# Attention scores as one 64-row by 128-column matmul each, in a kernel whose other matmuls are 64 by 32

## The chip, the cores and the metric

The kernel runs on one core of a Trainium2 chip. The metric is the device time of one execution in microseconds (us). A core has TensorE (PE, with its weight loads shown apart as PEld), VectorE (DVE), ScalarE (ACT), GpSimd (POOL) and SyncE (SP, which issues the DMAs). Matmul results go to PSUM, which here is one tensor `ps` of 128 partitions by 8 banks of 512 f32.

## The reference, cut to what matters

```python
xn = _layernorm(x)                                  # x: 1 x 2048 x 512, bf16
# attention, 32 heads of 16
scores = jnp.einsum("bhqd,bhkd->bhqk", q, k) * (Dh ** -0.5)
p = _softmax(scores, axis=-1)
o = jnp.einsum("bhqk,bhkd->bhqd", p, v)             # then @ wo
# feed-forward, F = 1792
gate = einsum(xn, W_gate); up = einsum(xn, W_up)
h = gate * (gate > 0) * up                          # then @ W_down
return x + attention(xn) + feed_forward(xn)
```

## The kernel before, in words

**Tiling.** The 2048 queries are cut into 4 blocks `c4` of 512, the 32 heads into 4 groups `gg` of 8, and each group into two sets `ee` of 4 heads. The 2048 keys are cut into 16 tiles `kt` of 128. `kT` holds the keys transposed: 128 partitions are the 8 heads of a group at 16 rows each. `qT` holds the queries with the rows of the other heads set to zero, so that a product over 64 rows (4 heads) gives the scores of one head: an operation takes half of the rows of the array, 64, and writes 128 keys by 512 queries to a PSUM bank.

**Scores.** `score` (L1180) is one such operation for one head, one key tile, one query block. It is done as four weight loads of 64 rows by 32 columns (`kload`, L1189) and four matmuls of 64 by 32 (`sc`, L1193) that write 32 partitions each of the same bank. There are 2048 of these operations, 1024 on each half of the rows.

**Exponentials.** Most key tiles go through ACT: two score operations, one on each half of the rows, fill two banks, and one ACTIVATE (L1252) turns them into probabilities in `ring`; that is a unit, and there are 720. The others (`quad`, L1203) go through DVE: four score operations, each evacuated by a TENSOR_SCALAR (L1211) into `qd` as the bits of an approximate exponential, with two shifted copies made by DVE (L1230) and POOL (L1226).

**Probability times value (PV).** `pv_stream` (L1143) multiplies `v_aug` (values, and a column of ones for the sum) with the probabilities, again as four loads and four matmuls of 64 by 32 for each half, accumulated in one bank.

**The rest.** Projections (`mm_chain`, L770, with `chain_part`, L749), the feed-forward (`glu`, L907) and the output rows (`out_rows`, L941) are woven in between as four loads and four matmuls of 64 by 32 on one half. At the start and at the end some matmuls use 128 rows: transposes (128x128, L720), fillers (128x128, L1267, and 128x32, L1272) that wait for nothing, the last output rows (128x32, L1089), and sums and spreads of the last normalisation (L1051, L1062).

**Order.** Every operation is registered with `G.op`, with an engine, a planned duration (216 ns for each TensorE operation of the halves), a priority and what it reads and writes. `Graph.run` places all of them once, before launch, and so fixes the order of each engine's queue. For TensorE it tracks the two halves of the rows apart and takes operations of mode "half" on both halves side by side; a change between the modes "half", "col" and "full" has a planned cost:

```python
    SWITCH = 107.0
```

`Graph.emit` (L373) writes the queues as instructions. For TensorE it remembers for each half which weights are loaded (`held`, by `wkey`) and leaves out a load where the same weights are there already (L382 to L389). A matmul whose weights were loaded by its own instruction goes through `matmul_loaded` (L99), which passes the tile size; so all these matmuls, scores and others, carry the line L101 in the profile. An operation is four instructions of that line.

Of the kernel before, what the change touches and what calls it, by code (L numbers as in the profile page):

```python
# [95 lines left out]
                 "load", "wsrc", "wkey", "wwaits")  # L96


def matmul_loaded(e, out, w, x, start, stop, at):  # L99

    return e.add_instruction(mybir.InstMatmult(  # L101
        name=e.bass.get_next_instruction_name(), engine=mybir.EngineType.PE, ins=[e.lower_ap(x), e.lower_ap(w)], outs=[e.lower_ap(out)],
        start_tensor_calc=start, stop_tensor_calc=stop, tile_size=(64, 32), tile_position=at, ldweights=False))


class Graph:
# [266 lines left out]
    def emit(self, nc, es):  # L373
# [5 lines left out]
        sems = {c: es.enter_context(nc.semaphore("s_" + c.lower())) for c in ("PE", "PEhi", "ACT", "DVE", "POOL")}  # L379
        known = {e: {} for e in self.ENGS}  # L380

        loads, held = {}, [None, None]  # L382
        for o in self.queue["PE"]:
            if o.load is None:
                held = [None, None]
            elif held[o.half] == o.wkey:
                o.load, o.wsrc = False, ()
            else:
                held[o.half] = o.wkey  # L389
# [16 lines left out]
        while left:  # L406
            moved = False
            for e in self.ENGS:
                q = self.queue[e]
                while pos[e] < len(q):  # L410
                    o = q[pos[e]]
                    if any(d.hb is None for d in o.deps):
                        break
                    k = known[e]
# [94 lines left out]
def bass_parallel_sum__mha_block__glu_gated_reglu__prompt_kernel(  # L509
# [14 lines left out]
    with ExitStack() as es:  # L524
        def sb(name, shape, dt):
            return es.enter_context(nc.sbuf_tensor(name, shape, dt))
# [22 lines left out]
        kT = sb("kT", [128, NGG, S], BF16)  # L549
        qT = sb("qT", [128, NQ, 4, 512], BF16)  # L550
# [17 lines left out]
        ps = es.enter_context(nc.psum_tensor("ps", [128, 8, 512], FP32))  # L568
# [180 lines left out]
        def chain_part(w, x, dst, half, flags):  # L749

            def fn(e):
                start, stop = flags()
                ww, xx, d, ins = w(), x(), dst(), None
                for j in range(4):
                    c = slice(32 * j, 32 * j + 32)
                    if half is None:
                        ins = e.matmul(d[c, :], ww[:, c], xx, start=start, stop=stop, tile_position=(0, 32 * j))
                    else:
                        ins = matmul_loaded(e, d[c, :], ww[rows, c], xx[rows], start, stop, (rows.start, 32 * j))
                return ins  # L760

            def load(e):
                for j in range(4):
                    e.ldweights(w()[rows, 32 * j:32 * j + 32], tile_position=(rows.start, 32 * j))  # L764
            rows = slice(0, 128) if half is None else slice(64 * half, 64 * half + 64)
            return fn, load if half is not None else None
# [116 lines left out]
        def key_tiles(gg, kt):  # L883
            return t_k0 if gg == kt == 0 else t_k[(gg, kt // 4)]
# [110 lines left out]
        for c4 in range(NB):  # L995
            rows = []
# [12 lines left out]
        at, rest = 40.0, sum(j[1] for j in seq[:-4])  # L1009
        for w, n, fn, lead in seq:  # L1010
            at = max(at, w)
# [131 lines left out]
        def pv_stream(key, kt, src, reads, u, prio):  # L1143
# [10 lines left out]
            for half in range(2):  # L1154
                rows = slice(64 * half, 64 * half + 64)

                def vs(j, rows=rows):
                    a = VW * (8 * gg + 2 * j + ee) - DH * ee
                    return v_flat[rows, kt, a:a + 32]

                def vload(e, half=half, vs=vs):
                    for j in range(4):
                        e.ldweights(vs(j), tile_position=(64 * half, 32 * j))  # L1163

                def pv(e, half=half, vs=vs, rows=rows):
                    ins = None
                    for j in range(4):
                        ins = matmul_loaded(e, ps[32 * j:32 * j + 32, BANK[t.slot], :], vs(j), src[j](rows), st[0] == 0, st[0] == st[1] - 1, (64 * half, 32 * j))
                    st[0] += 1
                    return ins  # L1170
                o = G.op("PE", 216, pv, reads=[t_vones, t_v[kt]] + reads, joins=[t], prio=prio, name="pv%d" % u, mode="half", half=half, bank=(t, 0), slack=PV_SLACK,
                         load=vload, weights=[t_vones, t_v[kt]], wkey=("v", gg, ee, kt))
                pv_ops[key].append(o)
# [6 lines left out]
        def score(key, j, t, bank, sub, u, prio, order, urgent, joins=(), after=None):  # L1180

            c4, gg, ee, kt = key
            half, p = j // 2, j % 2
            rows, tq = slice(64 * half, 64 * half + 64), q_slot[(c4, gg)]

            def ks(m):
                return kT[rows, gg, 128 * kt + 32 * m:128 * kt + 32 * m + 32]

            def kload(e):  # L1189
                for m in range(4):  # L1190
                    e.ldweights(ks(m), tile_position=(64 * half, 32 * m))  # L1191

            def sc(e):  # L1193
                ins = None
                for m in range(4):
                    ins = matmul_loaded(e, ps[32 * m:32 * m + 32, bank(), :], ks(m), qT[rows, tq.slot, 2 * p + ee, :], True, True, (64 * half, 32 * m))
                return ins
            tq.r.append(G.op("PE", 216, sc, reads=[t_q[(c4, gg, ee)][p], key_tiles(gg, kt)], joins=[t] + list(joins), prio=prio, order=order,
                             name="sc%d" % u, mode="half", half=half, bank=(t, sub), urgent=urgent, after=after,
                             load=kload, weights=[key_tiles(gg, kt)], wkey=("k", gg, kt)))  # L1200
            return G.ops[-1]
# [38 lines left out]
        for u, unit in enumerate(units):  # L1240
# [5 lines left out]
            key, p = unit[:4], unit[4]  # L1246
# [58 lines left out]
```

## Time and profile before

| what | before |
|---|---|
| median of 2 runs (lowest to highest) | 712.56 us (710.72 to 714.4) |
| the profiled execution | 710.57 us |
| its span | 708.8 us |
| mean granted TensorE clock | 0.998 |
| TensorE matmuls | 690.8 us busy, 22224 |
| TensorE weight loads | 378.5 us busy, 20965 |
| ACT | 669.3 us busy, 728 |
| DVE | 637.0 us busy, 1055 |
| POOL | 415.6 us busy, 358 |
| score matmuls (64*32) | 8192, with 8084 weight loads |

The span runs from the first to the last instruction of the profiled execution; its own time is a little longer. Busy is the union of the instructions' times on an engine. Matmuls are pipelined: a matmul of 512 columns is shown 0.38 us long though the next of its half starts earlier, so the pace is read from the starts. In a group's line come the source line, engine, operation, tensors, tile size (rows*columns), shape and count, then busy time, mean length of one in ns, and idle time of the engine before them with what ended it.

### The profile page before, as it was taken

Reading aid. Unit: us, or ns where it says so; the run is one execution under the profiler, and the core shown is the slowest. Engines: PE = TensorE matmul, PEld = TensorE weight load, DVE = VectorE, ACT = ScalarE, POOL = GpSimd, SP = SyncE. Lnnn points to the kernel's source line nnn. Section 1 sums busy time; section 2 is a strip of 40 time slices with the busy share of each in tenths; the row PEclk is TensorE's granted clock in tenths of the full one; section 3 lists DMA queues with packets and bytes.
Section 4 is the critical chain, followed back from the end, with each engine's and each line's share of the span. In section 5 each row is a group of like instructions: output and inputs, shape, how many; then the busy total and the mean of one; then the engine's idle time right before and its main releaser. Section 6 shows DMA issues by size and latency. Waiting matters only on the chain.

```text
span 708.8 us, 46867 instructions
## 1 busy us (share of the span) xinstructions
PE 690.8 (97%) x22224; PEld 378.5 (53%) x20965; DVE 637.0 (90%) x1055; ACT 669.3 (94%) x728; POOL 415.6 (59%) x358
## 2 busy tenths in 40 slices
PE   8989999999999999999999999999999999999996
PEld 4455555555445555555555555555555465555552
DVE  8766999999999988999999999799999989999873
ACT  5799999999999999999999999999999999999972
POOL 3203654756666547758647667576566766765641
PEclk9999999999999999999999999999999999999999
DMA  7322132243221113122221112232210122122011
GB/s 208 63 64 56 37 74 57 59 129 79 56 50 32 41 49 74 40 66 52 61 61 31 35 43 68 54 72 63 62 49 23 36 53 70 42 63 63 27 30 34
DMA packets 94893, 41.22 MB, mean 58 GB/s; under 512 B 77224, under 2 KB 90728, under 8 KB 94696
## 3 DMA queue, kind: packets, MB, share of 16 engines
q1 hardware_dynamic: 94696, 38.22, 21.3%
q8 instruction: 169, 2.77, 1.7%
q14 instruction: 28, 0.23, 0.1%
HBM read 31.06 MB, written 2.35 MB: 47 GB/s over the span
## 4 chain that ended last, share of the span: by engine, by line
PE 88%; DVE 4%; DMA 2%; ACT 2%; issue 1%; SPq 1%; POOL 1%; DVEq 0%; POOLq 0%
PE ps L101 85%; ACT ring L1252 2%; DVE qd L1211 2%; SPq L812 1%; DMA rb<-rec_scr 1%; PE ps L863 1%; DVE qd L1230 1%; PE ps L1267 1%; DMA xnT<-xn_sb 1%; DMA rec_scr<-rrec 0%; DMA x_sb<-oT 0%; PE ps L1089 0%; POOL oT L1131 0%; DVE o_sb L1110 0%; DVE v_aug L829 0%
## 5 line engine op out<-in xcount | busy, mean ns | idle before, releaser
L1252 ACT ACTIVATE ring<-ps 128x1024 bf16<-128x1024 f32 x720 | 664.2, 1100 | 17.8 <-PE ps L101 16.4
L101 PE MATMUL ps<-qT,kT 64*32 64x512 bf16 x8192 | 466.3, 376 | 4.2 <-ACT ring L1252 2.0
L1211 DVE TENSOR_SCALAR qd<-ps 128x512 int16<-128x512 f32 x608 | 396.3, 684 | 30.4 <-PE ps L101 26.4
L1226 POOL TENSOR_TENSOR qd<-qd,shift 128x512 int32<-128x512 int32 x272 | 277.0, 1040 | 203.8 <-DVE qd L1230 93.8
L101 PE MATMUL ps<-qd,v_aug 64*32 64x512 bf16 x3648 | 297.9, 375 | 1.8 <-issue 1.2
L1191 PEld LDWEIGHTS <-kT 64*32 64x32 bf16 x8084 | 172.4, 91 | 160.6 <-issue 77.6
L101 PE MATMUL ps<-ring,v_aug 64*32 64x512 bf16 x2880 | 249.9, 376 | 0.4
L1163 PEld LDWEIGHTS <-v_aug 64*32 64x32 bf16 x5376 | 130.5, 91 | 68.6 <-issue 26.2
L101 PE MATMUL ps<-xnT,wgs 64*32 64x512 bf16 x1792 | 135.5, 375 | 0.0
L101 PE MATMUL ps<-xnT,wus 64*32 64x512 bf16 x1792 | 134.6, 375 | 0.3 <-issue 0.2
L1230 DVE TENSOR_SCALAR qd<-qd 128x2048 int16<-128x2048 int16 x168 | 115.8, 701 | 5.6 <-PE ps L101 5.1
L1118 POOL TENSOR_TENSOR rrec<-rsum,minus 128x16 f32<-128x16 f32 x31 | 92.0, 2967 | 36.9 <-DMA rsum<-o_sb 36.9
L764 PEld LDWEIGHTS <-hT 64*32 64x32 bf16 x1792 | 43.1, 91 | 25.4 <-issue 5.9
L101 PE MATMUL ps<-Wd,hT 64*32 64x512 bf16 x768 | 55.8, 376 | 0.6 <-DVE qd L1211 0.3
L764 PEld LDWEIGHTS <-wus 64*32 64x32 bf16 x1792 | 43.5, 91 | 20.3 <-issue 4.0
L764 PEld LDWEIGHTS <-wgs 64*32 64x32 bf16 x1792 | 43.2, 91 | 16.1 <-issue 3.6
L101 PE MATMUL ps<-Wv,hT 64*32 64x512 bf16 x512 | 41.1, 376 | 0.4 <-issue 0.4
L927 DVE SCALAR_TENSOR_TENSOR hT<-ps,up_sb 128x512 bf16<-128x512 f32 x56 | 38.3, 685 | 2.8 <-PE ps L101 2.6
L101 PE MATMUL ps<-Wk,hT 64*32 64x512 bf16 x512 | 40.5, 375 | 0.0
L923 DVE COPY up_sb<-ps 128x512 f32<-128x512 f32 x56 | 38.3, 684 | 2.0 <-PE ps L101 1.9
L101 PE MATMUL ps<-xnT,Wk 64*32 64x512 bf16 x480 | 36.0, 375 | 2.6 <-issue 1.5
L101 PE MATMUL ps<-Wo_p,x_sb 64*32 64x512 bf16 x448 | 36.5, 376 | 0.4 <-issue 0.4
(73 smaller groups left out, 287.6 us busy)
## 6 DMA issues: line engine op xcount, KB each, us to landing
rb<-rec_scr SPq DMA_DIRECT2D x31, 256.0 KB
wus<-in_B_W_up_dram SPq DMA_DIRECT2D x56, 128.0 KB, 3.1
wgs<-in_B_W_gate_dram SPq DMA_DIRECT2D x56, 128.0 KB, 3.2
xr_sb<-in_A_x_dram SPq DMA_DIRECT2D x16, 128.0 KB, 3.3
out_dram<-xn_sb SPq DMA_DIRECT2D x16, 128.0 KB, 1.7
qT<-qf SPq DMA_DIRECT2D x120, 16.0 KB, 2.6
x_sb<-in_A_x_dram SPq DMA_DIRECT2D x8, 128.0 KB, 2.8
x_sb<-oT SPq DMA_DIRECT2D x60, 16.0 KB, 2.4
```

Of the source, the lines that this page charges most:

```text
L101: return e.add_instruction(mybir.InstMatmult(name=e.bass.get_next_instruction_name(), engine=mybir.EngineType.PE, ins=[e.lower_ap(x), e.lo ...
L764: e.ldweights(w()[rows, 32 * j:32 * j + 32], tile_position=(rows.start, 32 * j))
L812: dma(lambda e, v=v, r=r: e.dma_start(qT[r, tq.slot, v, :], qf[r, tf.slot, :]), 16, reads=[tf, t_qz], writes=[], joins=[tq], prio=prio + 0 ...
L923: G.op("DVE", 603, lambda e: e.tensor_copy(up_sb[:, tup.slot, :], bank_of(tu)), reads=[tu], writes=[tup], prio=-590)
L927: G.op("DVE", 603, lambda e: e.scalar_tensor_tensor(out=hT[:, th.slot, :], in0=bank_of(tg), scalar=0.0, in1=up_sb[:, tup.slot, :], op0=ALU ...
L1118: G.op("POOL", 3060, lambda e: e.tensor_tensor(rrec[:, par, :], rsum[:, par, :], minus[:], ALU.pow), reads=[ts, t_ones], writes=[trr], pri ...
L1163: e.ldweights(vs(j), tile_position=(64 * half, 32 * j))
L1191: e.ldweights(ks(m), tile_position=(64 * half, 32 * m))
L1211: G.op("DVE", 601, lambda e, j=j, tx=tx: e.tensor_scalar(qd[:, tq.slot, 512 * j:512 * j + 512], ps[:, BANK[tx.slot], :], IBIAS[3], 0.0, op ...
L1226: G.op("POOL", POOL_NS / POOL_PIECES + 60, lambda e, x=x, c=slice(i * m, i * m + m): e.tensor_tensor(x().bitcast(I32)[:, c], raw().bitcast ...
L1230: G.op("DVE", 600, lambda e, n=n, x=x: e.tensor_scalar(x(), raw(), float(SHIFTS[n + 1]), None, op0=ALU.add), reads=[ti, tq], writes=[t], p ...
L1252: exp_ops[u] = G.op("ACT", 904, lambda e, tr=tr, k0=k0: e.activation(ring[:, tr.slot, :, :], ps[:, 4 * k0:4 * k0 + 2, :], ACTF.Exp, scale= ...
```

## The change

The scores alone are made with a tile of 64 rows by 128 columns: one weight load of 128 keys, and one matmul that writes all 128 partitions of the bank. `matmul_loaded` gets the number of columns as an argument, with 32 for all other callers. `emit` forgets which weights are held on both halves wherever the queue passes from a score to another operation or back, so that the first operation on a half after it loads its weights anew. What the planner sees of each operation is as before.

```diff
-def matmul_loaded(e, out, w, x, start, stop, at):
+def matmul_loaded(e, out, w, x, start, stop, at, cols=32):
...
-        start_tensor_calc=start, stop_tensor_calc=stop, tile_size=(64, 32), tile_position=at, ldweights=False))
+        start_tensor_calc=start, stop_tensor_calc=stop, tile_size=(64, cols), tile_position=at, ldweights=False))
...
-        loads, held = {}, [None, None]
+        loads, held, size = {}, [None, None], None
         for o in self.queue["PE"]:
+            wide = isinstance(o.wkey, tuple) and o.wkey[0] == "k"
+            if wide != size:
+                held, size = [None, None], wide
             if o.load is None:
...
-            def ks(m):
-                return kT[rows, gg, 128 * kt + 32 * m:128 * kt + 32 * m + 32]
+            def ks():
+                return kT[rows, gg, 128 * kt:128 * kt + 128]
 
             def kload(e):
-                for m in range(4):
-                    e.ldweights(ks(m), tile_position=(64 * half, 32 * m))
+                e.ldweights(ks(), tile_position=(64 * half, 0))
 
             def sc(e):
-                ins = None
-                for m in range(4):
-                    ins = matmul_loaded(e, ps[32 * m:32 * m + 32, bank(), :], ks(m), qT[rows, tq.slot, 2 * p + ee, :], True, True, (64 * half, 32 * m))
-                return ins
+                return matmul_loaded(e, ps[:, bank(), :], ks(), qT[rows, tq.slot, 2 * p + ee, :], True, True, (64 * half, 0), 128)
```

## The prediction

> **What bounds the kernel now.** I read the page's busy table first, then its chain, then the costliest groups. All are lines of the page of before.
>
> ```profile
> PE 690.8 (97%) x22224; PEld 378.5 (53%) x20965; DVE 637.0 (90%) x1055; ACT 669.3 (94%) x728; POOL 415.6 (59%) x358
> ...
> PE 88%; DVE 4%; DMA 2%; ACT 2%; issue 1%; SPq 1%; POOL 1%; DVEq 0%; POOLq 0%
> ...
> L1252 ACT ACTIVATE ring<-ps 128x1024 bf16<-128x1024 f32 x720 | 664.2, 1100 | 17.8 <-PE ps L101 16.4
> L101 PE MATMUL ps<-qT,kT 64*32 64x512 bf16 x8192 | 466.3, 376 | 4.2 <-ACT ring L1252 2.0
> ...
> L101 PE MATMUL ps<-qd,v_aug 64*32 64x512 bf16 x3648 | 297.9, 375 | 1.8 <-issue 1.2
> L1191 PEld LDWEIGHTS <-kT 64*32 64x32 bf16 x8084 | 172.4, 91 | 160.6 <-issue 77.6
> ```
>
> TensorE (PE) carries 88% of the chain that ended last, though ACT and DVE are also over 90% busy. A busy PE is not a full PE, so its work must be counted in slots. The timeline shows how a slot looks (start, length, engine, line, shape, count):
>
> ```profile
> 299.70 0.38 PE L101 MATMUL ps<-xnT,wus 64*32 64x512 bf16 x4
> 299.71 0.38 PE L101 MATMUL ps<-ring,v_aug 64*32 64x512 bf16 x4
> 299.92 0.38 PE L101 MATMUL ps<-xnT,wus 64*32 64x512 bf16 x4
> 299.93 0.38 PE L101 MATMUL ps<-qd,v_aug 64*32 64x512 bf16 x4
> ...
> 300.36 0.38 PE L101 MATMUL ps<-ring,v_aug 64*32 64x512 bf16 x4
> 300.39 0.56 PE L101 MATMUL ps<-qT,kT 64*32 64x512 bf16 x8
> 300.61 0.38 PE L101 MATMUL ps<-xnT,wus 64*32 64x512 bf16 x4
> 300.79 0.38 PE L101 MATMUL ps<-qT,kT 64*32 64x512 bf16 x4
> 300.82 0.38 PE L101 MATMUL ps<-qd,v_aug 64*32 64x512 bf16 x4
> ```
>
> The array works as two halves of 64 rows. Four matmuls of 64x32 start together on a half and fill it; the half takes its next four 0.216 us later (299.70 to 299.92). The 0.38 us is length with latency, not pace. The halves run different things at the same time: a projection beside a probability-times-value (PV) product, or (300.61, 300.79) a score beside a projection. This sharing is what the change touches.
>
> **An account of before in slots.** The kernel has 2752 half-width operations per half, 1024 of them scores: 2752 x 0.2157 = 593.6 us of stream. Of the span of 708.8 us that leaves 115 us. By the stretches of the trace, from 60 to 680 us (20,268 matmuls, 8 to a slot, 546.5 us of stream) 73.5 us are lost between slots; the start, the end and the few other matmuls take the remaining 41.7.
>
> **The change, part by part.**
>
> *The stream.* One matmul of 128 columns streams the same 512 elements as four of 32 beside each other: still one slot on its half. No gain. 6144 matmul instructions go. The four starts of an operation lie some 5 ns apart (first to fourth record), so 1024 scores per half could give 0 to 5 us. I take 0, since the matmuls wait on "issue" for only 4.5 us in the whole trace.
>
> *The weight load.* 8084 loads of 91 ns, four beside each other, become at most 2048 of 128 columns; a 128-column load of the transposes is 98 ns in the trace. It hides under the previous slot of 216 ns as now. Taken as 0; without that cover it is 0.1 us per score, which is what the next term measures. The PV operations that skip a load because the weights are held (288 of 1632) will load again after each change of size: also inside the next term.
>
> *The change of tile size.* This is new: a size of 64x128 between sizes of 64x32. Before has 14 changes of size, at start and end. From the timeline of the end:
>
> ```profile
> 696.09 0.60 PE L101 MATMUL ps<-ring,v_aug 64*32 64x512 bf16 x8
> 696.62 0.40 PE L1089 MATMUL ps<-Wo_p,x_sb 128*32 128x512 bf16 x4
> ...
> 698.14 0.39 PE L1089 MATMUL ps<-Wo_l,x_sb 128*32 128x512 bf16 x4
> 698.46 0.39 PE L101 MATMUL ps<-ring,v_aug 64*32 64x512 bf16 x4
> 698.78 0.62 PE L1272 MATMUL ps<-zeros 128*32 128x512 bf16 x8
> ```
>
> Slots without a change follow at 0.216 us; those with one at 0.32 (698.14 to 698.46 to 698.78), and the two slots from 696.09 take 0.53. A change costs 0.104 us, load of the new weights included. These rows change the number of rows, ours only the columns. The nearest row for columns alone:
>
> ```profile
> 699.38 0.97 PEld L1051 LDWEIGHTS ps<-selp,o_sb 128*128 128x128 f32 x8 [0.47 <-DVE o_sb L1047]
> ...
> 700.36 0.10 PEld L1272 LDWEIGHTS ps<-zeros 128*32 128x32 bf16 x4
> ```
>
> The eight loads come every 0.112 us, the last at 700.15; the filler behind them waits for nothing and could load at 700.26, but does at 700.36: 0.10 us late, for 128 to 32 columns on the same rows. One instance, with small f32 matmuls, so weak; it says that columns count. The bounds are 0 and 0.104 us for each change; I take 0.104, the row it is nearest to.
>
> How many changes? The planner fixes TensorE's order before launch, and the diff alters no duration, mode, priority or dependence that it sees, so the order stays. Along that queue the 2048 scores fall into 1026 stretches (429 with one score on each half, 315 with a single score, 266 with three, 16 longer). With the other stretches that makes 2055 changes, 2041 more than now: 2041 x 0.104 = 212 us.
>
> *The sharing lost.* If a change empties the array, a score can no longer run beside a 64x32 product. Each stretch then takes as many slots as its fuller half: 1315 for the scores instead of 1024, and 2188 for the other 3456 operations instead of 1728. Together 3503 against 2752: 751 x 0.2157 = 162 us.
>
> *Issue.* In a stretch the second half starts 13 ns after the first (two groups of loads and matmuls, as at 12.46 us). About half of the stretches feel it: some 12 us.
>
> *What is given back.* Of the 73.5 us lost between slots, part is waiting for ACT, DVE and the other half, and that has more room when the slots spread. All or nothing of it: 0 to 73.5. I take half, 37 us. ACT starts an exponential every 0.904 us at its fastest, 720 x 0.904 = 651 us, so it stops being near the bound; a score then waits behind TensorE's own order. DVE, POOL and the DMA queues issue what they did and have more time for it. The wait of a score for its PSUM bank, with all of TensorE's queue behind it, should get shorter, since the bank was read 1.1 us after the score two units earlier and a unit will take about 1.4 us.
>
> Sum: 708.8 + 212 + 162 + 12 - 37 = 1058 us of span. The profiled execution took 710.57 us, 1.8 more than its span, and is 0.3% under the median of 712.56. Forecast 1060 us. Its own range: 1020 with all the loss given back, 1097 with none, 20 us either way for 10 ns on each change: 1000 to 1115.
>
> The Trainium skill, "TensorEngine Tiling (Array Packing)", Key Properties, lists 64x128 and 64x32 as separate modes and says that a change of mode, not of tile alone, drains TensorE. By it the sum above stands even for columns alone, where the trace has a single weak row; without any drain it would be some 710.
>
> **Rivals.**
>
> *Each half changes by itself.* A half that turns to 64x128 pays, the other goes on in 64x32. For it: the halves run unrelated work and differ in their start by any offset in the timeline. Against it: the changes that the trace shows always involve all rows, so it can't tell. A half has 1413 or 1471 changes in its own order: some 1442 x 0.104 = 150 us, no sharing lost, 0 to 73.5 given back: 786 to 860, say 840 us. The Trainium skill, "TensorE: Matmul & The Clock Gate", Part 3, speaks for it: it describes loads that overlap running matmuls as long as the row groups differ, a concurrency of each sub-array.
>
> *No cost at all (the other side).* The column width is only a mask, and 64x128 mixes freely with 64x32. Then nothing on the path changes: 705 to 716, say 711 us; and if the 73.5 us between slots come partly from issue, 12,000 instructions fewer at 1.6 ns each (the spacing of records in a group) would give up to 20 us back: 690. It decides from the point where a change costs below 5 ns. Against it are the 0.10 us at 700.36 and the 4.5 us of "issue" waits.
>
> *No two 64x128 matmuls at once.* If the two halves can't both run at this width, the scores take 2048 slots instead of 1315: 733 x 0.2157 = 158 us more, 1218 us. No row speaks for it.
>
> *The edit has no effect* would show as 64*32 scores; the tile size is passed directly, so I leave it out.
>
> **How the numbers follow.** Array emptied at each change: 0.63. Each half by itself: 0.16. No cost: 0.13, of which 0.04 is a gain over 2%. No two at once: 0.05. Something in between, mostly slower: 0.03. A difference of 2% is about what a measurement of this kernel can tell from none. Slower over 2%: 0.63 + 0.16 + 0.05 + 0.02 = 0.86; within 2%: 0.09 + 0.01 = 0.10; faster: 0.04. The range takes in the first two cases and what lies between and a little above, and leaves out "no cost" and most of "no two at once": 800 to 1150 us.
>
> **What would show it.** Right: 2048 matmuls of 64*128 in the groups; a score starting 0.32 us after the last other product and never inside the slot of one; PE over 90% of the chain, ACT's exponentials still some 0.9 us long at best but only about 60% to 75% busy, and fewer waits for ACT. A score that overlaps a 64*32 slot on the other half proves the first rival or the second: the first if the same half shows gaps of 0.32, the second if 0.216. Score pairs 0.2 us apart prove the third. I am wrong in the mechanism if the time is below 900 us, in a size only if it is between.

## The result and the profile after

The changed kernel takes 1013.62 us (median of 2 runs, 1013.57 to 1013.68) against 712.56 us: a ratio of 1.42, 95% interval 1.41 to 1.44. The profiled execution has a span of 1011.9 us at a granted clock of 0.997. The forecast was 1060 us.

From the page of the changed kernel, in the order of the lines shown of before (busy, chain, groups):

```profile
PE 1002.3 (99%) x16080; PEld 276.4 (27%) x15081; DVE 667.7 (66%) x1055; ACT 737.4 (73%) x728; POOL 417.2 (41%) x358
...
PE 98%; DVE 1%; ACT 1%; issue 0%; DVEq 0%; ACTq 0%
...
L1251 ACT ACTIVATE ring<-ps 128x1024 bf16<-128x1024 f32 x720 | 732.3, 1024 | 252.7 <-PE ps L101 241.0
...
L101 PE MATMUL ps<-qT,kT 64*128 64x512 bf16 x2048 | 462.3, 385 | 1.6 <-ACT ring L1251 0.9
...
L1193 PEld LDWEIGHTS <-kT 64*128 64x128 bf16 x2040 | 102.7, 93 | 380.1 <-issue 376.3
L1166 PEld LDWEIGHTS <-v_aug 64*32 64x32 bf16 x5536 | 108.9, 90 | 177.2 <-issue 157.5
```

TensorE has 6144 matmuls and 5900 loads fewer to do and is busy 311 us longer with it. It carries 98% of the chain instead of 88%. ACT waited 16.4 us for TensorE before and waits 241.0 now: nothing beside TensorE bounds the kernel any more. The new number to see is the idle time of the weight loads of the scores: 376 us ended by "issue", that is by nothing that the profile shows, against 77.6 before. Loads that used to slip under the running slot now stand still until the array is ready.

The timeline of the changed kernel shows why (start, length, engine, line, shape, count):

```profile
420.12 0.39 PE L101 MATMUL ps<-ring,v_aug 64*32 64x512 bf16 x4
420.13 0.39 PE L101 MATMUL ps<-xnT,wus 64*32 64x512 bf16 x4
420.34 0.38 PE L101 MATMUL ps<-qd,v_aug 64*32 64x512 bf16 x4
420.35 0.38 PE L101 MATMUL ps<-xnT,wus 64*32 64x512 bf16 x4
420.67 0.39 PE L101 MATMUL ps<-qT,kT 64*128 64x512 bf16 x1
420.99 0.39 PE L101 MATMUL ps<-xnT,wus 64*32 64x512 bf16 x4
421.30 0.39 PE L101 MATMUL ps<-qT,kT 64*128 64x512 bf16 x2
421.63 0.39 PE L101 MATMUL ps<-qd,v_aug 64*32 64x512 bf16 x4
421.64 0.39 PE L101 MATMUL ps<-xnT,wgs 64*32 64x512 bf16 x4
421.85 0.38 PE L101 MATMUL ps<-ring,v_aug 64*32 64x512 bf16 x4
```

Inside a stretch of one size the step is still 0.22 us (420.12 to 420.34). Across a change it is 0.32 (420.35 to 420.67 to 420.99 to 421.30 to 421.63). And the score at 420.67 stands alone, with the other half of the rows idle; so does the projection at 420.99. In before the other half went on with its own work under a score.

By the records of the whole trace: matmuls of the two widths on 64 rows change over 2047 times, and from the last start before a change to the first start after it takes 0.305 us at least and 0.322 us at most in 19 of 20 cases. All sum up to 645.1 us, mean 0.3151. The new weights are loaded at the end of that step: the first load of the new size starts 0.304 to 0.315 us after the last start of the old one in 9 of 10 cases, and its matmul some 0.006 us behind it. The load of the score at 420.67:

```profile
420.66 0.09 PEld L1193 LDWEIGHTS <-kT 64*128 64x128 bf16 x1 [0.42 <-issue]
```

By these records the price lies ahead of the load, not in its 0.09 us. No run changes the size without a new load, so a share of the load in the price is not ruled out.

### The profile page after: what moved, and what is told of

Its sections match the earlier page's. It is cut to its first block, busy times and chain, and to the rows that moved or that the text cites. A ratio compares the mean times of both kernels' runs of the same rounds, so it can differ in the third digit from the quotient of the medians.

```text
span 1011.9 us, 34839 instructions
## 1 busy us (share of the span) xinstructions
PE 1002.3 (99%) x16080; PEld 276.4 (27%) x15081; DVE 667.7 (66%) x1055; ACT 737.4 (73%) x728; POOL 417.2 (41%) x358
## 4 chain that ended last, share of the span: by engine, by line
PE 98%; DVE 1%; ACT 1%; issue 0%; DVEq 0%; ACTq 0%
PE ps L101 96%; ACT ring L1251 1%; PE ps L866 0%; PE ps L1266 0%; PE ps L1092 0%; DVE xn_sb L1083 0%; DVE xn_sb L701 0%; DVE xnT L739 0%; PE ps L760 0%; PE ps L1054 0%; PE ps L879 0%; PE ps L723 0%; PE ps L1271 0%; DVE v_aug L832 0%; DVE qd L1210 0%
## 5 line engine op out<-in xcount | busy, mean ns | idle before, releaser
L1251 ACT ACTIVATE ring<-ps 128x1024 bf16<-128x1024 f32 x720 | 732.3, 1024 | 252.7 <-PE ps L101 241.0
L1210 DVE TENSOR_SCALAR qd<-ps 128x512 int16<-128x512 f32 x608 | 413.4, 689 | 225.8 <-PE ps L101 223.0
L101 PE MATMUL ps<-qT,kT 64*128 64x512 bf16 x2048 | 462.3, 385 | 1.6 <-ACT ring L1251 0.9
L1193 PEld LDWEIGHTS <-kT 64*128 64x128 bf16 x2040 | 102.7, 93 | 380.1 <-issue 376.3
L1166 PEld LDWEIGHTS <-v_aug 64*32 64x32 bf16 x5536 | 108.9, 90 | 177.2 <-issue 157.5
L101 PE MATMUL ps<-xnT,wus 64*32 64x512 bf16 x1792 | 142.5, 379 | 0.0
L767 PEld LDWEIGHTS <-wgs 64*32 64x32 bf16 x1792 | 34.1, 89 | 45.8 <-issue 40.2
L767 PEld LDWEIGHTS <-wus 64*32 64x32 bf16 x1792 | 34.3, 89 | 43.2 <-issue 37.2
L767 PEld LDWEIGHTS <-hT 64*32 64x32 bf16 x1792 | 31.9, 90 | 35.6 <-issue 29.9
L101 PE MATMUL ps<-xnT,Wq 64*32 64x512 bf16 x480 | 38.1, 379 | 0.0
```

The costliest lines, as they stand in the source:

```text
L101: return e.add_instruction(mybir.InstMatmult(name=e.bass.get_next_instruction_name(), engine=mybir.EngineType.PE, ins=[e.lower_ap(x), e.lo ...
L1193: e.ldweights(ks(), tile_position=(64 * half, 0))
L1210: G.op("DVE", 601, lambda e, j=j, tx=tx: e.tensor_scalar(qd[:, tq.slot, 512 * j:512 * j + 512], ps[:, BANK[tx.slot], :], IBIAS[3], 0.0, op ...
L1251: exp_ops[u] = G.op("ACT", 904, lambda e, tr=tr, k0=k0: e.activation(ring[:, tr.slot, :, :], ps[:, 4 * k0:4 * k0 + 2, :], ACTF.Exp, scale= ...
```

## The experiments

**The price by itself.** A kernel of eight series of operations that wait for nothing:

```diff
...
+                for n in range(N):
+                    for half in range(2):
+                        op(e, ws["turns"], half, 32 if n % 2 else 128, n)
+                for n in range(N):
+                    op(e, ws["sides"], 0, 128, n)
+                    op(e, ws["sides"], 1, 32, n)
...
```

> This kernel leaves out the whole computation and runs eight series of TensorE operations that wait for nothing, 60 steps each; a step is an operation on each half of the rows (one half only in the last series), with its weight loads, told apart in the profile by the name of the weights. Time of a step in us by the theory that a change of tile size empties the whole array for 0.10 us: narrow (64x32 only) 0.216; wide (64x128 only) 0.216; turns (both halves wide, then both narrow) 0.32; sides (one half always wide, the other always narrow, in turn) 0.64, since each operation stands alone; c64 (64x64 only) 0.216; turns64 (64x64 in turn with 64x32) 0.32; pairs (two steps wide, two narrow) 0.27; oneside (one half alone, wide and narrow in turn) 0.32. If each half changes by itself: sides 0.216, the others as above. If two wide matmuls can't run at once: wide 0.43. If the wide weight load is not hidden: wide about 0.31, and turns no more than the mean of narrow and wide.

Measured by the starts, from the first step of a series to its last: wide 0.216 a step, turns 0.328, turns64 0.337, pairs 0.272, all as the emptied array would have it. Narrow (0.261) and c64 (0.238) began at half the clock, and narrow has one pause of 1.46 us besides; their later steps are 0.216. Sides is the series that decides. The weight loads, from its timeline:

```profile
56.57 0.09 PEld L34 LDWEIGHTS <-w_sides 64*32 64x32 bf16 x4 [0.23 <-issue]
56.89 0.09 PEld L34 LDWEIGHTS <-w_sides 64*128 64x128 bf16 x1 [0.23 <-issue]
57.21 0.09 PEld L34 LDWEIGHTS <-w_sides 64*32 64x32 bf16 x4 [0.23 <-issue]
57.53 0.09 PEld L34 LDWEIGHTS <-w_sides 64*128 64x128 bf16 x1 [0.23 <-issue]
...
71.15 0.10 PEld L34 LDWEIGHTS <-w_sides 64*32 64x32 bf16 x4 [0.43 <-issue]
71.69 0.10 PEld L34 LDWEIGHTS <-w_sides 64*128 64x128 bf16 x1 [0.44 <-issue]
```

Each half keeps its width throughout and never changes by itself, yet the two take turns at 0.32 us, 0.64 for both: these two widths don't run beside each other. That ends the theory that each half changes by itself. Two wide matmuls do run together (wide, 0.216), which ends the rival of 1218 us. From 60.4 us on the steps of sides are 0.54 us; that is the clock (last section).

**The loads by themselves.** Before, with the rule that forgets held weights kept:

```diff
-        loads, held = {}, [None, None]
+        loads, held, size = {}, [None, None], None
         for o in self.queue["PE"]:
+            wide = isinstance(o.wkey, tuple) and o.wkey[0] == "k"
+            if wide != size:
+                held, size = [None, None], wide
```

> All tiles are 64x32 as before; only the rule that held weights are forgotten between scores and other operations is kept from the change. If the change of tile size costs the time: 712 us, within 1% of before, since 54 to 300 more loads of 0.09 us lie under running slots. If the loads do: well above 712, up to the 1013 us of the changed kernel.

The median of 10 runs is 713.79 us against 713.51 of before, ratio 0.9999 (interval 0.9964 to 1.0034). Its group of PV loads shows the same 5536 as the changed kernel, against 5376 of before:

```profile
L1166 PEld LDWEIGHTS <-v_aug 64*32 64x32 bf16 x5536 | 133.9, 92 | 73.0 <-issue 29.3 <-DVE v_aug L832 2.0
```

More loads cost nothing as long as they lie under slots.

**Part of the scores wide.** Three kernels give the wide tile to some scores only, with the queue in the same order. Cut to the line that differs between them, here as in units; quads has `urgent == 1` and half0 `half == 0`:

```diff
...
+            wide = urgent == 2
...
```

> Only the 1440 scores for ACT's exponentials are 64x128; the 608 for DVE stay 64x32. Along TensorE's queue that makes 1437 changes of size and 3020 slots (before: 2752 slots; the full change: 2055 and 3503). If each change empties the array, with 635 us for 2752 slots, 0.216 us for each further slot and 0.105 us for each further change, as the full change measured: 635 + 58 + 149 = 842 us. If the cost goes by the number of wide scores: 712 + 0.70 x 301 = 924 us. If each half pays for itself, somewhere near that, 900 to 930 us.

> Only the 608 scores that DVE evacuates are 64x128; the 1440 for ACT stay 64x32. Along TensorE's queue: 1208 changes and 3305 slots. If a change empties the array: 635 + 119 + 125 = 880 us, more than with only ACT's 1440 scores wide, for fewer than half as many wide scores. If the cost goes by the number of wide scores: 712 + 0.30 x 301 = 801 us.

> Only the scores on half 0 of the rows (1024 of 2048) are 64x128; those on half 1 stay 64x32. If a change empties the whole array, a score on half 0 can no longer run beside one on half 1: 2031 changes and 3857 slots, 635 + 238 + 212 = 1085 us, longer than with all scores wide (1013 us). If the cost goes by the number of wide scores: about 863 us. If each half changes by itself: half 1 is undisturbed and half 0 pays what it does now, so no more than 1013 us.

The expected numbers are spans, since they are built on that of the changed kernel. Each kernel of the table but the last ran once.

| kernel | wide scores | changes on 64 rows | slots | expected, us | span, us |
|---|---|---|---|---|---|
| units | 1440 | 1429 | 3020 | 842 | 845.7 |
| quads | 608 | 1200 | 3305 | 880 | 888.7 |
| half0 | 1024 | 2023 | 3857 | 1085 | 1092.4 |
| the change | 2048 | 2047 | 3503 | fitted | 1011.9 |

The changes are counted in the traces, the slots along the queue. Half as many wide scores cost 80 us more than all of them, and 608 cost more than 1440. No theory that counts wide scores gives that order; changes and lost slots give it within 1%. The expectations take 0.105 us for a change; with the mean of 0.0994 measured in the changed kernel they come to 846, 885 and 1086 us, within 1% as well. The timeline of half0, matmuls and then two of its weight loads:

```profile
500.43 0.71 PE L101 MATMUL ps<-qT,kT 64*128 64x512 bf16 x5
500.76 0.39 PE L101 MATMUL ps<-qd,v_aug 64*32 64x512 bf16 x4
...
501.19 0.38 PE L101 MATMUL ps<-qT,kT 64*32 64x512 bf16 x4
```

```profile
500.43 0.09 PEld L1198 LDWEIGHTS <-kT 64*128 64x128 bf16 x1 [0.42 <-issue]
500.74 0.09 PEld L1201 LDWEIGHTS <-kT 64*32 64x32 bf16 x4 [0.23 <-issue]
```

The merged line of five at 500.43 is one wide score (its load at 500.43) and four narrow matmuls of the score on the other half, some 0.32 us later (their load at 500.74): a pair that ran side by side is now torn apart. In this run the granted clock was 0.5 for 27 us, from 848 to 875 us; at the steps of sides that is some 11 us of its 1092.

**Width 64.** Two matmuls of 64x64 for each score:

```diff
-                e.ldweights(ks(), tile_position=(64 * half, 0))
+                for m in range(2):
+                    e.ldweights(ks(m), tile_position=(64 * half, 64 * m))
```

> All scores as two matmuls of 64x64 instead of one of 64x128; the order and the number of changes are those of the full change. If any change of column size costs the same: 1013 us within 1%. If the price goes by the width, or by the load of 128 columns: between 712 and 1013, about 860 us.

1027.74 us (one run), 1.4% above the full change: a small miss. The price does not fall with the width. The 14 us more are there to see: from 64x64 to 64x32 the typical step is 0.333 us, against 0.321 from 64x128, and steps inside stretches of scores sum to 75.7 us against 69.3. Which part of the second load and matmul makes that was not tried.

**The planner told.** Scores get a planner's mode of their own:

```diff
-            if o.mode != "half" or pe["mode"] != "half":
+            if o.half is None or pe["mode"] != o.mode:
...
-                             name="sc%d" % u, mode="half", half=half, bank=(t, sub), urgent=urgent, after=after,
+                             name="sc%d" % u, mode="wide", half=half, bank=(t, sub), urgent=urgent, after=after,
...
```

> The full change, and the planner is told: scores have a mode of their own, so that it counts its 107 ns for a change between scores and other operations and no longer plans them side by side. Its queue has 1093 changes and 3027 slots instead of 2055 and 3503. If changes and lost sharing are the cost: at least 635 + 59 + 113 = 808 us, and above that what TensorE then waits for ACT, DVE and its own results, which the new order has not been seen to cost: 808 to 900 us, 850 most likely. If the cost goes by the wide scores alone: 1013 us.

> The order of the run before (the planner told of a mode for scores), but all tiles 64x32, so nothing changes size on the chip. What it takes less than that run is the price of the changes and of the lost sharing in one and the same order: 59 + 113 = 172 us at most, less what waits take their place. If the changes are the cost: 700 to 740 us, since the exponentials, at 0.904 us each, need 651 us and start late. If the order alone costs the time: as the run before.

917.88 us and 904.19 us, one run each. The first is 96 us better than the full change and 18 above its range; the second is far off: with no change of size left on the chip, the same order is still 190 us slower than before. So in this order changes and lost sharing make a difference of only 14 us (917.88 less 904.19), or at most some 7 more, since planned_narrow ran at half the clock for 27 us in all and planned for some 14. Where much of the rest is, the timeline of planned_narrow shows, TensorE first and then ACT:

```profile
421.59 0.38 PE L101 MATMUL ps<-xnT,wgs 64*32 64x512 bf16 x4
421.61 0.38 PE L101 MATMUL ps<-qd,v_aug 64*32 64x512 bf16 x4
422.29 0.40 PE L101 MATMUL ps<-qT,kT 64*32 64x512 bf16 x8 [0.30 <-ACT ring L1252]
422.51 0.38 PE L101 MATMUL ps<-xnT,Wq 64*32 64x512 bf16 x4
```

```profile
420.29 1.95 ACT L1252 ACTIVATE ring<-ps 128x1024 bf16<-128x1024 f32 x2
```

From 421.61 to 422.29 nothing starts, because a pair of scores is next in the queue and its bank is still being read by ACT, until 422.24; the products behind it in the queue start after it. Pauses like this, over 0.33 us between starts and ended by a score, sum to 135 us beyond a slot in this trace and to 10 us in before; in the trace of the wide version to some 54 us. There are over 500 of them in planned_narrow, and in nine of ten an exponential of ACT or an evacuation by DVE ended less than 0.08 us before the score started. So the pauses hold some 125 of the 190 us, and the rest stays open. The new order bunches scores, and the price of a change falls at least in part into waits that are there without it. All this is read from the traces; no run took the pauses away.

## Why the prediction was right, point by point

- **What bounds.** Right. TensorE's slots, with the rest far off: ACT's waits for TensorE rose by 225 us.
- **One slot for a wide score.** Right: wide steps of 0.216 us.
- **Loads hidden.** Right for their number (reload), and whatever share the load after a change has is inside the price.
- **The price of a change.** 2041 x 0.104 = 212 us was forecast. Measured 2047 x (0.3151 - 0.2157) = 203 us. The rows used changed the number of rows; the weak row at 700.36 was right that columns count alike.
- **The count.** 2055 changes were counted along the queue, those at start and end included; the trace has 2058. The trace of before has 11 of them, not 14, so that 2047 are new instead of 2041, which is under 1 us.
- **Sharing lost.** 162 us was forecast, and the same count of slots placed the three partial kernels within 1%.
- **Issue and what is given back.** This is the term that was mis-sized. 708.8 + 203 + 162 = 1074, and 1011.9 was measured: 62 us net were given back, against 25 (37 less 12). The trace of the change says where: its 1456 slots inside stretches take 339.8 us (69.3 and 270.5), 0.233 each, 26 us over 0.2157, and that holds issue and every remaining wait there. Of these 26 us, 22 lie between 60 and 980 us, so of the 73.5 us that before lost between slots in its middle some 51 went. The other 11 us came from the start, the end and the few other matmuls, where before lost 41.7 us and the changed kernel 30.5, and where the forecast took nothing back. A unit now has 1.41 us (1011.9 / 720) instead of 0.98, while ACT needs 0.904. That this is the room which the waits went into is argued; how the 73.5 us had been shared among ACT, DVE and the other half was not tried. "All of it" would have given 1021 us of span, nearer to the 1011.9, but in part by luck: it gives back 22 us too many in the middle, against a price 9 us too high, 12 us of issue counted beside those 22, and 11 us of the ends left out. The prediction's "1020" and "1097" mix the two times: its sum gives 1021 and 1095 us of span, 1023 and 1097 of time.
- **Rivals.** Each half by itself fell with sides and half0; no cost at all, and no two wide at once, with the result and with series.

The Trainium skill, "TensorEngine Tiling (Array Packing)", Key Properties, has the rule that a change of tiling mode drains TensorE (the sizes that the prediction names are listed just ahead of it, in Available Configurations). The traces agree for every pair tried here: 64x32 with 64x128 and with 64x64, 0.32 us from start to start instead of 0.216. Its line beside it that tiles operate independently was seen here between tiles of one size alone: in sides, two halves of different width never started less than 0.305 us apart.

## What to carry to other kernels

Count changes of tile size along TensorE's queue, as one counts slots: here each cost 0.10 us for the whole array, whichever half asked for it, and broke up work that shared the array. Fewer and wider instructions win nothing where the stream of columns is the limit, and a size used on one half of the rows only can be dearer than no use or use everywhere (half0), since it breaks up pairs. Used for some scores on both halves, it was cheaper than everywhere (units, quads). When a change stretches the bounding engine, expect part of the waits that other engines caused to go (62 us here), and check an order meant to save a price by running it without the price.

## What the runs showed of the hardware that was not expected

A TensorE that is shown busy all the time can have its clock halved. In series, with PE busy throughout, the clock was 1.00 while both halves streamed together at steps of 0.33 us (turns, 35 to 55 us) and fell to 0.50 some 5 us into sides, at 60.4 us, where only one half streams at a time. The windows of series, for 35.3 to 54.5, 55 to 59 and 70 to 115 us (stretch, its length, PE busy, granted clock, DMA share, GB/s):

```profile
35.30:54.50 19.20, 19.20 (x294) 1.00 0.01 2
55.00:59.00 4.00, 4.00 (x39) 1.00 0.00 0
70.00:115.00 45.00, 45.00 (x211) 0.50 0.00 0
```

The steps go from 0.320 to 0.538 us with it, and oneside, which uses one half alone, falls the same way. The kernels have little of it: the changed kernel 3.4 us from 790.6 us on, half0 its 27 us, and planned_narrow 27 us too, with one size only. How little work it takes for the clock to fall was not tried.
